# Freeing 8 KB of tables, more buffers for two kinds of tile, a new order for the first weight slab and spaced loads, in a fused long-convolution and gated-MLP training step

## Chip, cores and metric

One core of one Trainium2 chip. The time is the device time of one execution in microseconds (us). The kernel before took 2044.09 us (median of 3 runs, 2042.13 to 2049.22) when the prediction was made.

## The reference

Forward and backward pass of one block, for 2048 positions, 1024 channels and an MLP width of 3584, all in bf16. The output and the gradients of nine inputs are wanted.

```python
xn = layernorm(q)
k_shift = sum of 4 shifted copies of k, each times a column of shift_k
kv = k_shift * v
y = irfft(rfft(pad(kv)) * rfft(pad(ssm_k)))[:2048] + kv * ssm_D      # long convolution
s = xn * y
h = (xn @ w_gate) * (xn @ w_up)
g = silu(h @ w_down)
out = q + s * g
# and jax.vjp of this with respect to q, k, v, shift_k, ssm_k, ssm_D, w_gate, w_up, w_down
```

## The kernel before

TensorE does the large products. The convolution runs beside them: its Fourier transforms are small matmuls with table tiles (TF for one direction, TI for the other) plus additions on VectorE, fed to the engines a piece at a time while the matmul loops go on. `tt` is a two-input VectorE instruction, `ld` a load issued by SyncE, `sta` a store issued by ScalarE, and `st` and `cld` a store and a load issued by GpSimd. Tiles come from pools. In the profile's lines a name that ends in d (DYFd, HFd, DGd) is a tensor in device memory, a name that begins with ps is a tile in PSUM, and U stands for any tile of the pool from which dgu comes.

```python
TI = tip.tile([P, 2, 8, 2, P], BF16, name="TI")      # 8 KB a partition
TF = tfp.tile([P, 2, 8, 2, P], BF16, name="TF")      # 8 KB; the second halves are needed only in the forward convolution
# ... the first two weight slabs (chunks of 1, 1, 2, 4, 4, 4 row blocks):
for i, (b0, n, x4) in enumerate(xs):
    # ... layer norm of the next chunk
    for sl in range(2):
        gu_unit(sl, b0, n, slabs[sl], nop)
# ... backward, gradient of h for one half of a slab:
def dh_half(k, wdt):
    for g in range(2):
        dht = bg.tile([P, 4, SLW], BF16, name="dht", bufs=3)
        for e in range(2):
            # ... 16 matmuls into ps
            nc.scalar.copy(out=dht[:, 2 * e:2 * e + 2]..., in_=ps[:])
            flush(2)                                  # runs stores deferred earlier
            btick(1)                                  # lets the backward convolution go on a little
        tt(dgu[:, bs], dgu[:, bs], dht..., MUL)
    def store():                                      # two DMAs from ScalarE's queue
        for a in range(2):
            sta(DGd[...], dgu[:, :, a, :])
    defer(store)
# ... backward convolution:
def conv_backward():
    cx, cs = pool("d_cx", 2), pool("d_cs", 1)
    yield from dy_forward(cx, cs)      # 8 units: load kvx and dyx, transform into DX (in d_cs), store DYFd[ds] <- DX
    cs.release(); cx.release(); tfp.release()
    ab, cs, ew = pool("e_ab", 1), pool("e_cs", 1), pool("e_ew", 1)
    # A and B: two tiles of 8 KB each
    load_a(0)                          # A <- DYFd[0]
    load_b(0)                          # B <- HFd[0]
    for n in range(16):                # product of A and B, inverse transform, tail
        yield from staggered(main(n), tl, 5.0)
        tl = tail(n)
```

Of the kernel before, what the change touches and what calls it, by code (L numbers as in the profile page):

```python
# [13 lines left out]
BF16 = mybir.dt.bfloat16  # L14
# [5 lines left out]
def build_kernel(  # L20
# [11 lines left out]
    nc = tc.nc  # L32
    P = 128
# [6 lines left out]
    SLW = 256  # L40
# [17 lines left out]
    V = nc.vector  # L58
# [66 lines left out]
    Wbc = const.tile([P, 4, D], BF16, name="Wbc")  # L125

    tip = tc.alloc_tile_pool(name="tip", bufs=1)
    TI = tip.tile([P, 2, 8, 2, P], BF16, name="TI")
    tfp = tc.alloc_tile_pool(name="tfp", bufs=1)
    TF = tfp.tile([P, 2, 8, 2, P], BF16, name="TF")  # L130
    T4 = [TF[:, 0], TF[:, 1]]

    def zero_rows(bsb):
        zr = bsb.tile([8, 8, P], BF16, name="zr")
# [31 lines left out]
    def build_tables(psp, tg, ang):  # L166

        m = ang
        for q in range(2):
            dst = T4[q].rearrange("p r k f -> p k r f")  # L170
            sc = 2.0 * np.pi / 4096.0
            mm = tg.tile([P, 8, P], I32, name="mm")
            if q == 0:
                V.tensor_single_scalar(mm[:], m[:], 4095, ALU.bitwise_and)
            else:
                nc.gpsimd.iota(mm[:], pattern=[[512 * q, 8], [0, P]], base=0, channel_multiplier=0)
                tt(mm[:], m[:], mm[:], ADD)
                V.tensor_single_scalar(mm[:], mm[:], 4095, ALU.bitwise_and)
            nc.scalar.activation(dst[:, 1], mm[:], ACT.Sin, bias=negpi[:], scale=sc)
            ab_ = tg.tile([P, 8, P], F32, name="ab_")  # L180
            nc.scalar.activation(ab_[:], mm[:], ACT.Abs, bias=negpi[:], scale=sc)
            nc.scalar.activation(dst[:, 0], ab_[:], ACT.Sin, bias=mhpi[:], scale=1.0)
        for j in range(2):
            for rq in range(2):
                ps = psp.tile([P, 4, 2, P], BF16, name="tr")
                for i in range(4):
                    for k in range(2):
                        nc.tensor.transpose(ps[:, i, k, :], T4[j][:, 4 * rq + i, k, :], ident[:])
                V.tensor_copy(TI[:, j, 4 * rq:4 * rq + 4], ps[:])


    def pr(t, i, j):
# [154 lines left out]
    def gseg(G, r, j, k):  # L347
        a = r % 4
        return G[:, 4 * a + 2 * j + (1 - k if a == 3 else k), :]
# [37 lines left out]
    def inv8_rows(G, psp, rp):  # L387
        ps = psp.tile([P, 2, 256], F32, name="psY")
        for i in range(2):
            r = 2 * rp + i  # L390
            for k in range(2):
                nc.tensor.matmul(ps[:, i, :], TI[:, 0, r, k, :], G[:, 2 * r + k, :], start=(k == 0), stop=(k == 1))
        return ps

    def inv_rows(G, psp, rp):

        ps = psp.tile([P, 2, 256], F32, name="psY")
        for i in range(2):
            r = 2 * rp + i
            n = 0  # L400
            for j in range(2):
                for k in range(2):
                    nc.tensor.matmul(ps[:, i, :], TI[:, j, r, k, :], gseg(G, r, j, k),
                                     start=(n == 0), stop=(n == 3))
                    n += 1
        return ps
# [172 lines left out]
    def conv_forward():  # L579
# [96 lines left out]
        kst.release()  # L676
        cs.release()
        cx.release()

    F_TOTAL = 4 * 20.0 + 8 * (0.2 + 2 * FWD4_W + 1.4 + 1.2 + PROD_W + INV_W + 1.6)  # L680
    nop = lambda: None
# [21 lines left out]
    for i, (b0, n, x4) in enumerate(xs):  # L703
        if i + 1 < len(xs):
            with tc.issue_after(last.ins):
                last, root, xst = layer_norm(*xs[i + 1])
        for sl in range(2):
            gu_unit(sl, b0, n, slabs[sl], nop)
            if i in (3, 4):
                with tc.issue_after(gu_mm[0].ins):  # L710
                    for j in ((3, 4), (2,), (1,), (0,))[2 * (i - 3) + sl]:
                        bcast(j)
        if i == len(xs) - 1:
            with tc.issue_after(root.ins):
                build_tables(ps_st, tg, ang)
# [184 lines left out]
    def dh_tail(ds, G, ew):  # L900
        hr = ew.tile([P, 2, 8, P], BF16, name="yl")
        ho = ew.tile([P, 2, P, 8], BF16, name="ho")
        for c in range(2):
            for rq in range(2):
                ps = ps_y4[0].tile([P, 4, P], F32, name="psY")
                for i in range(4):
                    r = 4 * rq + i
                    for k in range(2):
                        nc.tensor.matmul(ps[:, i, :], G[:, 2 * r + k, c * P:(c + 1) * P], TI[:, 0, r, k, :],
                                         start=(k == 0), stop=(k == 1))  # L910
                nc.scalar.activation(hr[:, c, 4 * rq:4 * rq + 4], ps[:], ACT.Copy, scale=WSC)
                yield 0.1
        nc.gpsimd.tensor_copy(ho[:], hr[:].rearrange("p c r u -> p c u r"))
        st(o_dssmk[ds * P:(ds + 1) * P, :], ho[:].rearrange("p c u r -> p (c u r)"))
        yield 0.1

    def dk_units(ew, psp):
        def load(i):
            ds, c = divmod(i, 2)
            kh = ew.tile([P, 11, P], BF16, name="kh")  # L920
            cld_k(kh[:], c, ds)
            dk = ew.tile([P, 11, P], BF16, name="dkh")
            src = DKSHd[ds]
            cld(dk[:], bass.AP(src.tensor, src.offset + 1024 * c * P, [[8 * P, P], [P, 11], [1, P]]))
            return kh, dk

        kh, dk = load(0)
        yield 2
        for i in range(16):
            ds, c = divmod(i, 2)  # L930
            dsl = slice(ds * P, (ds + 1) * P)
            wb = lambda j: Wbc[:, j:j + 1, dsl].to_broadcast([P, 8, P])
            acc = ew.tile([P, 8, P], BF16, name="dka")
            tt(acc[:], dk[:, 3:11, :], wb(3), MUL)
            for j in (2, 1, 0):
                prod = ew.tile([P, 8, P], BF16, name="dkp")
                tt(prod[:], dk[:, j:j + 8, :], wb(j), MUL)
                tt(acc[:], acc[:], prod[:], ADD)
                yield 1
            st(o_dk[:, c, :, dsl], acc[:])  # L940
            if c == 0:
                ps = psp.tile([P, 4, 64], F32, name="psdk")
            for r in range(8):
                for j in (slice(0, 64), slice(64, 128)):
                    nc.tensor.matmul(ps[j], dk[:, r, j], kh[:, r:r + 4, j],
                                     start=(c == 0 and r == 0), stop=(c == 1 and r == 7))
            yield 1
            if i < 15:
                kh, dk = load(i + 1)
            if c == 1:  # L950
                dt_ = ew.tile([P, 4, 64], F32, name="dt2")
                tt(dt_[:], ps[:], diag[:].unsqueeze(1).to_broadcast([P, 4, 64]), MUL)
                dr_ = ew.tile([P, 4], F32, name="dr2")
                V.tensor_reduce(dr_[:], dt_[:], AX.X, ADD)
                V.tensor_copy(dsko[:, ds, ::-1], dr_[:])
            yield 2
        st(o_dshk.rearrange("(c p) j -> p c j", p=P), dsko[:])
    DK_TOTAL = 2 + 16 * 6

# [122 lines left out]
    def dh_half(k, wdt):  # L1082

        sl, hf = divmod(k, 2)
        dgu = DGU[k]
        for g in range(2):
            bs = slice(4 * g, 4 * g + 4)
            dht = bg.tile([P, 4, SLW], BF16, name="dht", bufs=3)
            for e in range(2):
                ps = ps_b.tile([P, 512], F32, name="psb")  # L1090
                for x in range(2):
                    b = 4 * g + 2 * e + x
                    for dc in range(DC):
                        nc.tensor.matmul(ps[:, x * SLW:(x + 1) * SLW], DBMT[2 * hf + g][:, dc, (b % 4) * P:(b % 4 + 1) * P],  # L1094
                                         wdt[:, dc, :], start=(dc == 0), stop=(dc == DC - 1))
                nc.scalar.copy(out=dht[:, 2 * e:2 * e + 2].rearrange("p b f -> p (b f)"), in_=ps[:])  # L1096
                flush(2)
                btick(1)
            with tc.high_priority(60):
                tt(dgu[:, bs], dgu[:, bs], dht[:].unsqueeze(2).to_broadcast([P, 4, 2, SLW]), MUL)  # L1100

        def store():
            fs = slice(sl % 2 * SLW, sl % 2 * SLW + SLW)
            for a in range(2):
                sta(DGd[sl // 2, a, 1024 * hf:1024 * hf + 1024, fs].rearrange("(b u) f -> u b f", u=P), dgu[:, :, a, :])
        defer(store)
        return dgu
# [49 lines left out]
    for p_ in (bg, bw):  # L1157
        p_.release()
    gd2 = pool("gd2", 1, side="right")
    wo = pool("wo", 4, side="right")  # L1160



# [199 lines left out]
```

## Time and profile before

| stage (where it starts) | us in the profile before |
|---|---|
| layer norm, slabs 0 and 1, start of slab 2, forward convolution | 0 to 569.0 |
| down projection | 569.0 to 767.0 |
| gradient of h, gradients of gate and up weights, backward convolution | 767.0 to 1426.7 |
| gradient of the down weight | 1426.7 to 1626.1 |
| gradient of x | 1626.1 to 2030.0, tail to 2039.6 |

The marks are the start of the first instruction of each stage on its main tile. The prediction shows the busy times by stage and the waits. Columns of single profile lines: start, duration, engine, instruction, idle time ahead of it and what ended that.

```profile
966.67 0.55 POOL L65 DMA_DIRECT2D DYFd<-DX  x1 [17.63 <-DVE DX L242]
967.45 0.54 POOL L65 DMA_DIRECT2D A<-DYFd  x1 [0.24 <-issue]
967.98 0.54 POOL L65 DMA_DIRECT2D B<-HFd  x1
968.51 0.53 POOL L65 DMA_DIRECT2D A<-DYFd  x1
977.30 0.53 POOL L65 DMA_DIRECT2D B<-HFd  x1 [8.27 <-DMA DYFd<-DX]
```

### The profile page before, as it was taken

What the parts mean: (1) busy time and instruction counts of PE and PEld (TensorE: products, weight loads), DVE (VectorE), ACT (ScalarE), POOL (GpSimd) and SP (SyncE); (2) the same over time, 40 slices, a digit from 0 to 9 for tenths busy, and PEclk for the clock granted to TensorE, in tenths of its full rate; (3) what the DMA queues carried; (4) which work ended last, traced back from release to release, by engine and by line L of the source; (5) the groups of instructions that cost most, each with busy time, mean ns of one, the idle gap of its engine ahead of it and who ended that gap; (6) DMA issues with size and microseconds to landing.
All of it is one profiled execution on the core that took longest, in us unless ns stands there. A gap on an engine that the chain in (4) does not pass through costs nothing.

```text
span 2039.6 us, 28672 instructions
## 1 busy us (share of the span) xinstructions
PE 1953.3 (96%) x11345; PEld 1053.9 (52%) x11530; DVE 1485.6 (73%) x2007; ACT 607.2 (30%) x956; POOL 341.8 (17%) x499
## 2 busy tenths in 40 slices
PE   6999999999999999999998999999999999999998
PEld 3455555555544446666565555565444444444443
DVE  7789999999836555888899899998968024444343
ACT  4644444444432233322222222222222101111112
POOL 3322222221112111000122111112121001111100
PEclk9999999999999999999999999999999999999999
DMA  9686766558699988766889778866996989393921
GB/s 302 233 289 209 249 219 229 196 199 276 213 304 291 292 282 277 228 210 172 296 246 250 224 221 265 249 202 223 244 234 167 219 207 225 102 219 92 232 69 57
DMA packets 468711, 454.43 MB, mean 223 GB/s; under 512 B 249456, under 2 KB 393624, under 8 KB 454624
## 3 DMA queue, kind: packets, MB, share of 16 engines
q1 hardware_dynamic: 324240, 190.08, 36.6%
q0 software_dynamic: 45200, 189.08, 27.4%
q10 hardware_dynamic: 99136, 73.42, 11.5%
q8 instruction: 90, 1.47, 0.3%
q14 instruction: 45, 0.37, 0.1%
HBM read 208.15 MB, written 194.02 MB: 197 GB/s over the span
## 4 chain that ended last, share of the span: by engine, by line
PE 60%; DVE 22%; issue 9%; DMA 6%; POOL 1%; ACT 1%; ACTq 0%; SPq 0%; DVEq 0%; POOLq 0%
PE psx L1235 19%; PE psbm L969 9%; PE psb L1212 9%; PE psb L1113 9%; DVE W L198 6%; DVE m L198 6%; PE psg L556 6%; PE psb L1094 3%; DVE HX L198 2%; DVE U L198 1%; DVE KX L198 1%; DMA B<-HFd 1%; DMA dyl<-DYd 1%; DVE A L198 1%; DVE B L198 1%
## 5 line engine op out<-in xcount | busy, mean ns | idle before, releaser
L556 PE MATMUL psg<-wslab,U 128*128 128x512 bf16 x1732 | 408.1, 382 | 11.8 <-ACT U L530 3.6
L1113 PE MATMUL psb<-U,U 128*128 128x512 bf16 x1745 | 399.9, 384 | 11.8 <-ACT dht L1096 5.4
L1235 PE MATMUL psx<-U,dgut 128*128 128x512 bf16 x1503 | 332.4, 379 | 2.8 <-issue 1.4
L1113 PEld LDWEIGHTS <-U 128*128 128x128 bf16 x1792 | 176.8, 99 | 216.1 <-issue 19.6
L1235 PEld LDWEIGHTS <-dgut 128*128 128x128 bf16 x1792 | 173.8, 98 | 211.1 <-issue 3.7
L556 PEld LDWEIGHTS <-U 128*128 128x128 bf16 x1792 | 173.6, 98 | 195.8 <-issue 12.6
L1094 PE MATMUL psb<-wdt,U 128*128 128x256 bf16 x1792 | 203.8, 274 | 10.8 <-ACT dht L1096 9.6
L558 ACT CAST gut<-psg 128x512 bf16<-128x512 f32 x224 | 131.2, 587 | 228.3 <-PE psg L556 212.0
L1212 PE MATMUL psb<-U,U 128*128 128x512 bf16 x876 | 194.8, 379 | 1.1
L1094 PEld LDWEIGHTS <-U 128*128 128x128 bf16 x1792 | 175.8, 98 | 34.6 <-issue 11.4
L969 PE MATMUL psbm<-U,ht 128*128 128x512 bf16 x768 | 168.9, 379 | 0.8
L1117 ACT CAST wb<-psb 128x512 bf16<-128x512 f32 x112 | 65.6, 586 | 317.0 <-PE psb L1113 229.0
L198 DVE TENSOR_TENSOR W<-W 128x1024 f32<-128x1024 f32 (+1 forms) x144 | 142.8, 1010 | 2.8
L198 DVE TENSOR_TENSOR m<-A,B 128x1024 bf16<-128x1024 bf16 (+1 forms) x160 | 116.6, 793 | 32.9 <-issue 23.3
L1212 PEld LDWEIGHTS <-U 128*128 128x128 bf16 x896 | 87.1, 98 | 102.4
L198 DVE TENSOR_TENSOR dka<-dkh,Wbc 128x1024 bf16<-128x1024 bf16 x16 | 11.1, 692 | 163.2 <-DMA dkh<-DKSHd 163.2
L969 PEld LDWEIGHTS <-ht 128*128 128x128 bf16 x784 | 76.6, 98 | 91.8
L1258 ACT ACTIVATE dx_t<-dxn 128x1024 bf16<-128x1024 f32 (+1 forms) x17 | 17.1, 1007 | 339.1 <-DVE dxn L198 285.8
L1096 ACT CAST dht<-psb 128x512 bf16<-128x512 f32 x112 | 65.0, 587 | 152.7 <-PE psb L1094 103.8
L198 DVE TENSOR_TENSOR W<-W,psP 128x512 f32<-128x512 f32 x128 | 81.0, 692 | 8.6 <-ACT W L228 6.7
L198 DVE TENSOR_TENSOR U<-U,dht 128x2048 bf16<-128x2048 bf16 x56 | 70.4, 1258 | 21.5 <-ACT dht L1096 21.5
L1214 ACT CAST wbs<-psb 128x512 bf16<-128x512 f32 x56 | 32.8, 586 | 159.5 <-PE psb L1212 142.4
(233 smaller groups left out, 2335.3 us busy)
## 6 DMA issues: line engine op xcount, KB each, us to landing
U<-GUd SPq DMA_DIRECT2D x28, 1024.0 KB, 7.2
DGd<-U ACTq DMA_DIRECT2D x56, 512.0 KB, 6.6
GUd<-gut ACTq DMA_DIRECT2D x54, 512.0 KB, 4.8
A<-DYFd POOLq DMA_DIRECT2D x16, 1024.0 KB, 5.5
U<-Hd SPq DMA_DIRECT2D x15, 1024.0 KB, 6.1
out_dram<-wb ACTq DMA_DIRECT2D x224, 64.0 KB, 3.3
Hd<-hN POOLq DMA_DIRECT2D x54, 256.0 KB, 4.0
HTd<-hT POOLq DMA_DIRECT2D x54, 256.0 KB, 4.2
```

What stands on the lines that cost most here:

```text
L198: V.tensor_tensor(o, a, b, op)
L556: gu_mm[0] = nc.tensor.matmul(ps[:], XNT[q][:, dc, qi * P:(qi + 1) * P], w[:, dc].rearrange("p a f -> p (a f)"), start=(dc == 0), stop=(dc ...
L558: nc.scalar.copy(out=gut[:, i].rearrange("p a f -> p (a f)"), in_=ps[:])
L969: nc.tensor.matmul(ps[:, dh * 512:(dh + 1) * 512], ht(fc)[:, i * P:(i + 1) * P], WD[fc // 4][:, fc % 4, dh * 512:(dh + 1) * 512], start=(f ...
L1094: nc.tensor.matmul(ps[:, x * SLW:(x + 1) * SLW], DBMT[2 * hf + g][:, dc, (b % 4) * P:(b % 4 + 1) * P], wdt[:, dc, :], start=(dc == 0), sto ...
L1096: nc.scalar.copy(out=dht[:, 2 * e:2 * e + 2].rearrange("p b f -> p (b f)"), in_=ps[:])
L1113: nc.tensor.matmul(ps[:], XN[b // 4][:, b % 4, dc * P:(dc + 1) * P], dgus[b // 8][:, b % 8].rearrange("p a f -> p (a f)"), start=(b == 0), ...
L1117: nc.scalar.copy(out=wb[:].rearrange("p a f -> p (a f)"), in_=ps[:])
L1212: nc.tensor.matmul(ps[:], h[:, b, f * P:(f + 1) * P], DBM[b // 4][:, b % 4, dh * 512:(dh + 1) * 512], start=(b == 0), stop=(b == NB - 1))
L1214: nc.scalar.copy(out=wbs[:, dh * 512:(dh + 1) * 512], in_=ps[:])
L1235: nc.tensor.matmul(ps[:, dh * 512:(dh + 1) * 512], t[n][:, f, i * P:(i + 1) * P], WGU[n][:, f, dh * 512:(dh + 1) * 512], start=(n == 0 and ...
L1258: nc.scalar.activation(dx_t[:, cl], dxn[:, cl], ACT.Identity, accum_out=sums[:, 0, h:h + 1])
```

## The change

Its intent: the second halves of TI and TF are given to a pool of their own (tfo) that is released after the forward convolution, which frees 8 KB a partition; the room goes to two more buffers for dht and two for the stores of the down gradient (wbs). The two units of slab 0 are put ahead of the last units of slab 1, so that its buffer comes free sooner. The work units of the dk part are weighted anew, so that a load has more time before its first use.

```diff
-    TI = tip.tile([P, 2, 8, 2, P], BF16, name="TI")
+    TI = [tip.tile([P, 8, 2, P], BF16, name="TI0")]
     tfp = tc.alloc_tile_pool(name="tfp", bufs=1)
-    TF = tfp.tile([P, 2, 8, 2, P], BF16, name="TF")
-    T4 = [TF[:, 0], TF[:, 1]]
+    T4 = [tfp.tile([P, 8, 2, P], BF16, name="TF0")[:]]
+    tfo = tc.alloc_tile_pool(name="tfo", bufs=1)
+    TI.append(tfo.tile([P, 8, 2, P], BF16, name="TI1"))
+    T4.append(tfo.tile([P, 8, 2, P], BF16, name="TF1")[:])
 ...  (each TI[:, j, ...] becomes TI[j][:, ...])
         cx.release()
+        tfo.release()
 ...
-        for sl in range(2):
-            gu_unit(sl, b0, n, slabs[sl], nop)
-            if i in (3, 4):
+        for sl, c in ([(0, i), (1, i)], [(0, i)], [(0, i), (1, i - 1), (1, i)])[max(0, i - len(xs) + 3)]:
+            gu_unit(sl, xs[c][0], xs[c][1], slabs[sl], nop)
+            if c in (3, 4):
 ...  (dk: yields of 1, 1 and 2 become 0.5, 0.5 and 4)
-            dht = bg.tile([P, 4, SLW], BF16, name="dht", bufs=3)
+            dht = bg.tile([P, 4, SLW], BF16, name="dht", bufs=5)
 ...
-    wo = pool("wo", 4, side="right")
+    wo = pool("wo", 6, side="right")
```

More of the change, by code (lines that the diff above doesn't have):

```diff
@@ L188, in build_tables @@
                         nc.tensor.transpose(ps[:, i, k, :], T4[j][:, 4 * rq + i, k, :], ident[:])
-                V.tensor_copy(TI[:, j, 4 * rq:4 * rq + 4], ps[:])
+                V.tensor_copy(TI[j][:, 4 * rq:4 * rq + 4], ps[:])
     def pr(t, i, j):
@@ L391, in inv8_rows @@
             for k in range(2):
-                nc.tensor.matmul(ps[:, i, :], TI[:, 0, r, k, :], G[:, 2 * r + k, :], start=(k == 0), stop=(k == 1))
+                nc.tensor.matmul(ps[:, i, :], TI[0][:, r, k, :], G[:, 2 * r + k, :], start=(k == 0), stop=(k == 1))
         return ps
@@ L402, in inv_rows @@
                 for k in range(2):
-                    nc.tensor.matmul(ps[:, i, :], TI[:, j, r, k, :], gseg(G, r, j, k),
+                    nc.tensor.matmul(ps[:, i, :], TI[j][:, r, k, :], gseg(G, r, j, k),
                                      start=(n == 0), stop=(n == 3))
@@ L706, in build_kernel @@
                 last, root, xst = layer_norm(*xs[i + 1])
-        for sl in range(2):
-            gu_unit(sl, b0, n, slabs[sl], nop)
-            if i in (3, 4):
+        for sl, c in ([(0, i), (1, i)], [(0, i)], [(0, i), (1, i - 1), (1, i)])[max(0, i - len(xs) + 3)]:
+            gu_unit(sl, xs[c][0], xs[c][1], slabs[sl], nop)
+            if c in (3, 4):
                 with tc.issue_after(gu_mm[0].ins):
-                    for j in ((3, 4), (2,), (1,), (0,))[2 * (i - 3) + sl]:
+                    for j in ((3, 4), (2,), (1,), (0,))[2 * (c - 3) + sl]:
                         bcast(j)
@@ L908, in dh_tail @@
                     for k in range(2):
-                        nc.tensor.matmul(ps[:, i, :], G[:, 2 * r + k, c * P:(c + 1) * P], TI[:, 0, r, k, :],
+                        nc.tensor.matmul(ps[:, i, :], G[:, 2 * r + k, c * P:(c + 1) * P], TI[0][:, r, k, :],
                                          start=(k == 0), stop=(k == 1))
@@ L938, in dk_units @@
                 tt(acc[:], acc[:], prod[:], ADD)
-                yield 1
+                yield 0.5
             st(o_dk[:, c, :, dsl], acc[:])
@@ L946, in dk_units @@
                                      start=(c == 0 and r == 0), stop=(c == 1 and r == 7))
-            yield 1
+            yield 0.5
             if i < 15:
@@ L955, in dk_units @@
                 V.tensor_copy(dsko[:, ds, ::-1], dr_[:])
-            yield 2
+            yield 4
         st(o_dshk.rearrange("(c p) j -> p c j", p=P), dsko[:])
```

## The prediction

> **What bounds the kernel now.** I read the page's busy shares first, then the busy time of each engine by stage, then the list of waits on TensorE, then the order of instructions around the three largest gaps. From the page:
>
> ```profile
> PE 1953.3 (96%) x11345; PEld 1053.9 (52%) x11530; DVE 1485.6 (73%) x2007; ACT 607.2 (30%) x956; POOL 341.8 (17%) x499
> ```
>
> TensorE is busy for 1953.3 of 2039.6 us, so only 86.3 us of idle time can be won, plus whatever is lost to matmuls that run slower after a gap. The table by stage (columns: stretch, its length, busy time of PE, PEld, DVE, ACT, POOL, granted clock, DMA share, GB/s) says where that idle time lies. I cut the stages at the layer norm with the first two weight slabs, the start of slab 2, the other twelve slabs with the forward convolution, the down projection, the gradients of h and of gate and up with the backward convolution, the gradient of down, the gradient of x, and the tail:
>
> ```profile
> 0.00:96.40 96.40, 77.11 (x467) 37.90 (x474) 69.11 (x164) 59.52 (x88) 33.47 (x59) 1.00 0.80 262
> 96.40:116.00 19.60, 16.07 (x83) 7.77 (x85) 15.62 (x17) 5.93 (x10) 7.47 (x12) 0.91 1.05 344
> 116.00:569.40 453.40, 433.43 (x2702) 248.66 (x2753) 424.37 (x566) 217.26 (x344) 96.76 (x148) 1.00 0.66 229
> 569.40:765.00 195.60, 193.51 (x900) 88.80 (x918) 105.58 (x167) 51.69 (x51) 39.35 (x62) 1.00 0.95 292
> 765.00:1423.00 658.00, 630.19 (x4153) 387.76 (x4200) 580.12 (x729) 171.82 (x302) 97.55 (x141) 0.98 0.76 234
> 1423.00:1626.00 203.00, 201.94 (x1047) 96.96 (x1065) 131.07 (x151) 43.26 (x77) 28.68 (x20) 1.00 0.92 220
> 1626.00:2030.00 404.00, 400.75 (x2003) 186.02 (x2038) 155.23 (x206) 54.72 (x80) 38.53 (x61) 1.00 0.68 154
> ```
>
> Length minus PE busy: 19.3, 3.5, 20.0, 2.1, 27.8, 1.1 and 3.3 us; the tail of 9.6 us holds another 9.3. The two stages of the four edits that come last (down's gradient, x's gradient) have 4.4 us of idle between them. The stage with the gradient of h has most, and the granted clock is below one there and at the start of slab 2. The waits on TensorE:
>
> ```profile
> PE psb L1094 <- ACT dht L1096: 9.6, 2, 8.2
> PE psY L403 <- DVE HX L198: 9.0, 8, 2.0
> ...
> PE psb L1113 <- ACT dht L1096: 5.4, 1, 5.4
> ...
> PE psg L556 <- DMA wslab<-in_B_w_gate_dram: 3.3, 1, 3.3
> ```
>
> So what the change aims at on the path is 9.6 + 5.4 us behind ScalarE's copy into dht and 3.3 us behind one slab load.
>
> **What the Trainium skill says, and whether the trace agrees.** "TensorE: Matmul & The Clock Gate", Part 1 (the HAM clock gate), says that an idle window of about 3.4 us sends the array back to half clock and that about 3.4 us of work brings it back. The trace agrees: after the 5.43 us gap at 1170 fifteen records of 512 columns take from 1175.7 to 1181.8 us, 6.1 us, where warm ones are 0.216 us apart (49 in 10.74 us on the chain) and would need 3.2: 2.9 us lost beside the gap. "PSUM — Partial Sum Buffer", Engine vs sequencer instructions, says the queues of ScalarE and VectorE are strict FIFO; the ScalarE lines below agree, as four results sit in or wait for PSUM behind a store. "Perfetto Trace Analysis", Identifying Performance Opportunities, says that a gap that repeats on the engine that should be saturated can mean too few buffers. Here I doubt that reading, as I show next. "DMA: Bandwidth & Descriptors", Queues, rings and completion order, says each DMA engine takes turns among its queues; slab 2's load, in company with two 512 KB copies of k, takes 11.8 us, against a median of 7.1 for the 28 slab loads.
>
> **The change part by part.**
>
> First slab sooner. Before, the blocks of the last chunk follow the order slab 0 chunk 4, slab 1 chunk 4, slab 0 chunk 5, slab 1 chunk 5; slab 0's buffer comes free only at 87.3 us, and its successor is issued then:
>
> ```profile
> 87.32 0.39 SPq L480 DMA_DIRECT2D wslab<-in_B_w_up_dram  x1
> 87.75 0.59 SPq L480 DMA_DIRECT2D wslab<-in_B_w_gate_dram  x1
> ```
>
> It lands at 99.55; TensorE has run out at 96.4. After, both slab 0 units come first. A unit of four blocks is 32 matmuls, 32 x 0.216 = 6.9 us (with its transposes about 7.5), so the load starts near 80 and lands near 92 even at 11.8 us. The 3.25 us gap goes. Behind it, eight matmuls and eight transposes take 3.6 us where 2.2 would do: 1.4 us more. 4.7 us in sum. But from 116 us VectorE is busy 424.4 of 453.4 us, and TensorE's small gaps there are waits for it (9.0 us for HX). VectorE must also start the convolution sooner for TensorE to keep its lead; it idles 3.7 us near 103 for a store of shifted k that competes with the slab load, so I expect it to move most of the way. I put 4.0 us.
>
> Five dht buffers. Round the 8.19 us gap ScalarE and VectorE do this:
>
> ```profile
> 1110.16 0.59 ACT L1096 CAST dht<-psb 128x512 bf16<-128x512 f32 x1 [1.16 <-PE psb L1094]
> 1122.48 0.39 ACTq L68 DMA_DIRECT2D DGd<-U  x1
> 1122.91 0.59 ACT L1096 CAST dht<-psb 128x512 bf16<-128x512 f32 x1 [12.17 <-DVE U L198]
> ```
>
> ```profile
> 1112.43 1.23 DVE L198 TENSOR_TENSOR dyl<-dyl,Dbc 128x2048 bf16<-128x2048 bf16 x1 [4.15 <-DMA dyl<-DYd]
> 1113.57 2.28 DVE L198 TENSOR_TENSOR W<-A 128x2048 f32<-128x2048 bf16 x1
> ...
> 1118.29 1.22 DVE L198 TENSOR_TENSOR U<-U,dht 128x2048 bf16<-128x2048 bf16 x1
> ```
>
> The fifth cast does not wait for a dht buffer: with three, it takes the one whose product was made a whole slab earlier. It stands in ScalarE's queue behind the store of the product (DGd), which needs the second product of VectorE, done at 1122.45; and VectorE is late because of a load of dy. The same order (casts, store, cast) stands at the 5.43 us gap. Two more buffers remove the wait of the seventh cast for the first product, which this store already covers. They help only if the program's order around the store changes with them. If the store moves behind the casts, TensorE would go on to the weight gradients at 1117 and still need the product that ends at 1122.45 for its twelfth block, some 4 us of waiting in place of 8.2; at the other gap, where the second product ends at 1174.6 and TensorE would want it at 1170.3 + 12 x 0.216 = 1172.9, about 1.7 in place of 5.4. With the slow clocks behind the gaps (1.5 + 2.9 us) and the 1.4 us gap at 1309 that is 4.2 + 3.7 + 4.4 + 1.4 = 13.7 us at best. I give it somewhat under one half: 6.0 us.
>
> More down-store buffers: the gradient of down idles 1.1 us in 203. Worth 0, at most 1 us.
>
> dk's loads spaced. VectorE waits 163.2 us for dkh, the largest wait of the kernel, but TensorE idles 3.3 us in that stage of 404 us. The pump turns 98 units in about 196 x 1.73 = 339 us, 3.46 us a unit; the first product moves from two units after its load (6.9 us) to four (13.8 us), beyond the longest landing of 12.3 us. The wait should fall a great deal and the time not at all. The last 9.6 us hold no dk work. Worth 0.
>
> Sum: 4.0 + 6.0 + 0.5 (the small waits) = 10.5 us, from 2044.1 to 2033.6.
>
> **The rivals.** (1) The order of ScalarE's queue stays, the two long gaps stay: then only the slab's 4 us remain, 2040. For it speaks the store at 1122.48; against it, that a larger buffer count lets the instruction order be drawn up anew. (2) VectorE becomes the bound: in the convolution stages it is at 94% and 88%. Then TensorE's earlier start turns into longer waits for HX, and moved products meet later DMA loads: 2044, or with an unlucky order 2050. For it speaks the 9.0 us of HX waits in eight equal parts, one for each slice of channels; against it, that VectorE has ended its convolution near 553 us, some 15 us before TensorE ends that stage. (3) The new order also heals the gaps that no edit names: the 7.84 us for which a store holds ScalarE's queue at 784 us (3.7 us idle and 3.1 of slow clock), the 2.0 us at 994 with 1.9 of slow clock. Then the time would be near 2020.
>
> **Range and chances.** All idle time but the first 8 us and the tail is 69 us, and faster by over 2% would need 41 of it; none of the edits reaches that. Slower by over 2% would need an order much worse than this one in a kernel whose idle time is spread thin. Range 2020 to 2045: the lower end is rival 3, the upper is rival 2.
>
> **What would show it.** Slab 2's load issued near 80 us and no TensorE wait for it: step one right. DVE's first product of the convolution no earlier than 118 us would make it worth nothing. The waits of psb for dht gone while the DGd store still stands between casts would show me wrong on the queue; gaps of 5 to 8 us still there with DGd at their end would show me right, and the time near 2040. VectorE's wait for dkh below 60 us with PE idle still near 3 us in the last stage: the dk step right. An idle sum of the stage from 765 us above 28 us would make the whole prediction too low.

## More of the kernel before

Pools on the left side of SBUF form a stack that grows upwards, pools on the right one that grows downwards, and a pool's address is wherever the stack stands when it is opened.

```profile
970.39 1.23 DVE L198 TENSOR_TENSOR U<-U,dht 128x2048 bf16<-128x2048 bf16 x1 [4.01 <-ACT dht L1096]
973.88 1.23 DVE L198 TENSOR_TENSOR U<-U,dht 128x2048 bf16<-128x2048 bf16 x1 [2.27 <-ACT dht L1096]
977.38 1.22 DVE L198 TENSOR_TENSOR U<-U,dht 128x2048 bf16<-128x2048 bf16 x1 [2.27 <-ACT dht L1096]
982.21 3.63 DVE L198 TENSOR_TENSOR m<-A,B 128x2048 bf16<-128x2048 bf16 x5 [3.61 <-DMA B<-HFd]
```

The first B is asked for at 967.98 and used at 982.21. The second B, at 977.30, waits 8.27 us for the last store of DX. Nothing in the program's data joins B and DX: that wait is about the room they lie in.

## The result, and the profile after

The changed kernel took 2059.85 us (median of 4 runs, 2057.57 to 2061.37); the kernel before took 2045.21 us in the same rounds (4 runs, 2042.13 to 2049.22). The ratio is 1.0069, with a 95% interval of 1.0048 to 1.0091. All ratios here are the mean time of one kernel's fast runs over the mean of the other's fast runs of the same rounds, so not quite the ratio of the medians quoted. The change is within 2%, but it is slower, where 10.5 us faster was predicted, and it lies 15 us above the range's upper end.

The marks of the two profiled runs, in us:

| | down projection | gradient of h | down gradient | gradient of x | length of the stage from "gradient of h" |
|---|---|---|---|---|---|
| before | 569.0 | 767.0 | 1426.7 | 1626.1 | 659.7 |
| after | 571.2 | 769.1 | 1443.8 | 1643.2 | 674.7 |

Of 17.1 us by which the gradient of x starts later, 15.0 arise in the stage with the gradient of h. The table by stage of the changed kernel (columns as in the prediction's) puts that down to idle time of TensorE:

```profile
96.40:116.00 19.60, 19.41 (x140) 11.29 (x141) 14.36 (x15) 8.56 (x13) 6.57 (x10) 1.00 0.99 321
116.00:571.60 455.60, 433.29 (x2679) 247.30 (x2728) 431.90 (x573) 215.28 (x341) 98.22 (x150) 1.00 0.66 229
...
767.20:1440.10 672.90, 630.41 (x4153) 387.93 (x4200) 580.03 (x729) 171.21 (x302) 96.78 (x141) 0.97 0.76 229
```

In the third line TensorE is busy for 630.41 us, as before (630.19), and idle for 672.90 - 630.41 = 42.5 us, before 27.8: 14.7 us more. The list of waits on TensorE names where (columns: line, releaser, us in total, times, longest):

```profile
PE psb L1117 <- ACT wb L1121: 14.5, 1, 14.5
...
PE psb L1098 <- ACT dht L1100: 8.3, 2, 7.6
...
PE psY L394 <- DVE B L244: 5.6, 1, 5.6
PE psb L1117 <- ACT dht L1100: 4.7, 3, 4.0
```

The waits behind dht, which the change was to remove, are still there (8.3 + 4.7 for 9.6 + 5.4). New is one wait of 14.5 us behind ScalarE's cast into wb, the tile in which a block of a weight gradient is stored. It is followed back through four engines. TensorE, then ScalarE, then VectorE, then GpSimd's queue, of the changed kernel:

```profile
1008.91 12.98 PE L1117 MATMUL psb<-U,U 128*128 128x512 bf16 x47 [14.51 <-ACT wb L1121]
```

```profile
1007.21 1.02 ACTq L68 DMA_DIRECT2D DGd<-U  x2
1008.28 0.58 ACT L1121 CAST wb<-psb 128x512 bf16<-128x512 f32 x1 [23.61 <-DMA out_dram<-wb]
```

```profile
977.76 1.23 DVE L200 TENSOR_TENSOR U<-U,dht 128x2048 bf16<-128x2048 bf16 x1 [2.27 <-ACT dht L1100]
1000.00 3.63 DVE L200 TENSOR_TENSOR m<-A,B 128x2048 bf16<-128x2048 bf16 x5 [21.02 <-DMA B<-HFd]
1003.56 1.28 DVE L200 TENSOR_TENSOR m<-m 128x1024 bf16<-128x1024 bf16 x2
1004.76 1.28 DVE L200 TENSOR_TENSOR A<-m 128x1024 bf16<-128x1024 bf16 x2
1005.96 1.22 DVE L200 TENSOR_TENSOR U<-U,dht 128x2048 bf16<-128x2048 bf16 x1
```

```profile
967.05 0.54 POOL L65 DMA_DIRECT2D DYFd<-DX  x1 [17.64 <-DVE DX L244]
967.59 0.53 POOL L65 DMA_DIRECT2D A<-DYFd  x1
977.65 0.53 POOL L65 DMA_DIRECT2D B<-HFd  x1 [9.53 <-DMA DYFd<-DX]
978.17 0.53 POOL L65 DMA_DIRECT2D A<-DYFd  x1
978.69 0.53 POOL L65 DMA_DIRECT2D B<-HFd  x1
979.24 0.53 POOL L65 DMA_DIRECT2D dyl<-DYd  x1
979.88 2.98 POOL L65 DMA_DIRECT2D vl<-in_A_v_dram  x4
```

Read from below. The load of the first B now waits 9.53 us for the last store of DX, and is issued at 977.65 for 967.98. Behind it seven loads (A, B, dyl and four of vl) go out in one burst. B is usable only at 1000.00, 22 us after its issue, for 14 us before, and VectorE stands still for 21.02 us in front of a product that needs it, where it waited 3.61. Behind that product, in VectorE's order, stands the fourth product of U with dht (1005.96); the store of U (DGd, 1007.21) needs it; ScalarE's casts stand behind the store (1008.28; the profile puts the wait down to an old store of wb, but the DGd store just ahead of the cast ran 1 us before, right after the product's end at 1007.18); and TensorE's next matmuls need a PSUM tile that those casts empty (1008.91).

Why B waits for DX is shown by no profile but by the addresses in the compiled programs (bytes in a partition):

```
tile               before                          after
TI / TF            28288-36480 / 36480-44672       28288-32384 / 32384-36480
dyx (2 buffers)    52864-61056                     44672-52864
DX                 61056-69248                     52864-61056
A, first           36480-44672                     32384-40576
B, first           52864-61056  (on dyx)           48768-56960  (on dyx and DX)
B, second          61056-69248  (on DX)            56960-65152  (on DX)
```

The pools of the eight forward units stand on top of TI and TF, so they move down by the freed 8 KB. The pool of A and B stands in place of TF itself, so it moves down by 4 KB. Against each other they are shifted by 4 KB, and the first B comes to lie partly on DX. Before, only the second B did, whose product follows the first without a gap. The load of B into room that the store of DX still reads waits for that store: 9.53 us here.

### The profile page after: what moved, and what is told of

The parts are those of the page before. It is cut to its first block, busy times and chain, and to the rows that moved or that the text cites. A ratio compares the mean times of both kernels' runs of the same rounds, so it can differ in the third digit from the quotient of the medians.

```text
span 2056.8 us, 28643 instructions
## 1 busy us (share of the span) xinstructions
PE 1957.1 (95%) x11346; PEld 1055.1 (51%) x11530; DVE 1488.2 (72%) x2007; ACT 606.8 (30%) x956; POOL 340.2 (17%) x499
## 4 chain that ended last, share of the span: by engine, by line
PE 57%; DVE 24%; issue 11%; DMA 6%; POOL 1%; ACT 1%; ACTq 1%; SPq 0%; DVEq 0%; POOLq 0%
PE psx L1239 18%; PE psbm L973 9%; PE psb L1216 9%; DVE W L200 7%; PE psg L558 6%; DVE m L200 6%; PE psb L1117 5%; DVE HX L200 3%; PE psb L1098 3%; DVE U L200 2%; DVE KX L200 1%; DMA vl<-in_A_v_dram 1%; DMA dyl<-DYd 1%; PE psY L405 1%; DVE B L200 1%
## 5 line engine op out<-in xcount | busy, mean ns | idle before, releaser
L1117 PE MATMUL psb<-U,U 128*128 128x512 bf16 x1745 | 399.9, 384 | 23.5 <-ACT wb L1121 14.5
L1098 PEld LDWEIGHTS <-U 128*128 128x128 bf16 x1792 | 175.8, 98 | 33.3 <-issue 10.1
L200 DVE TENSOR_TENSOR dka<-dkh,Wbc 128x1024 bf16<-128x1024 bf16 x16 | 11.1, 692 | 183.1 <-DMA dkh<-DKSHd 183.1
L1262 ACT ACTIVATE dx_t<-dxn 128x1024 bf16<-128x1024 f32 (+1 forms) x17 | 17.1, 1007 | 338.5 <-DVE dxn L200 297.7
```

Of the source, the lines that this page charges most:

```text
L200: V.tensor_tensor(o, a, b, op)
L1098: nc.tensor.matmul(ps[:, x * SLW:(x + 1) * SLW], DBMT[2 * hf + g][:, dc, (b % 4) * P:(b % 4 + 1) * P], wdt[:, dc, :], start=(dc == 0), sto ...
L1117: nc.tensor.matmul(ps[:], XN[b // 4][:, b % 4, dc * P:(dc + 1) * P], dgus[b // 8][:, b % 8].rearrange("p a f -> p (a f)"), start=(b == 0), ...
```

## The experiments

Medians are in us. Before ran at 2047.97 (11 runs) beside e1 to e4, at 2046.14 (11) beside e5 to e8, and at 2049.28 (11) beside e9 and e10; each of these groups ran on another chip, so ratios are compared across groups and not medians. "Stage" is the length of the stage with the gradient of h in the profiled run, by the marks of the first table.

| run | median (runs) | ratio, 95% interval | stage |
|---|---|---|---|
| before | 2045.21 (4) | 1 | 659.7 |
| after | 2059.85 (4) | 1.0069 (1.0048 to 1.0091) | 674.7 |
| e1, before, tables split only | 2063.49 (4) | 1.0064 (1.0032 to 1.0096) | 671.0 |
| e2, after, 4 KB of padding | 2051.75 (4) | 1.0008 (0.9971 to 1.0045) | 666.8 |
| e3, after, three dht buffers | 2064.00 (4) | 1.0057 (1.0018 to 1.0095) | 673.2 |
| e4, before, slab order only | 2046.77 (6) | 0.9986 (0.9960 to 1.0012) | 660.2 |
| e5, after, DX elsewhere | 2043.44 (6) | 0.9982 (0.9959 to 1.0004) | 657.9 |
| e6, e5 with a later DGd store | 2045.23 (6) | 0.9987 (0.9961 to 1.0012) | 658.9 |
| e7, e6 with three dht buffers | 2043.84 (6) | 0.9985 (0.9964 to 1.0007) | 661.5 |
| e8, before, dk and wbs edits only | 2045.12 (4) | 0.9987 (0.9961 to 1.0013) | 663.2 |
| e9, three dht buffers, first A and B loaded ahead | 2036.42 (6) | 0.9947 (0.9919 to 0.9976) | 653.7 |
| e10, e9 with a later DGd store | 2031.58 (6) | 0.9928 (0.9895 to 0.9961) | 643.6 |

The theory was that the shift of the tiles makes the loss. The rivals were that one of the named edits does: another order of instructions from five dht buffers, or VectorE's new order from the slab edit.

**e1: the kernel before with nothing but the split tables.**

```diff
  before, with TI and TF cut in halves and tfo released, as in the change; dht 3 buffers, wo 4, slab and dk as before
```

> The kernel before with the tables alone split in halves and the second halves freed early; four table and loop edits of the change left out otherwise, and the built order of the instructions is that of before but for three table copies on VectorE. Theory P (placement): the freed room moves every tile behind the tables down by 4 or 8 KB, so that the first buffer for the spectra (B) no longer lies where the dead loads of dy lay but on DX, whose last store must be read out first; the load of B is issued about 9 us later, in one burst with four others. P expects about 2059 us, ratio 1.006 to 1.009, with the 14 us wait of the weight gradients behind ScalarE near 994 us. Rival Q (the five buffers or the other loop edits cost the time): 2045 us, ratio 1.000.

The order of instructions is that of the kernel before on four engines, and differs in 3 lines on VectorE. The whole loss is there: ratio 1.0064. The list of waits of this run in the stage, on TensorE:

```profile
PE psb L1097 <- ACT dht L1099: 8.4, 2, 7.7
PE psb L1116 <- ACT wb L1120: 7.1, 1, 7.1
PE psY L394 <- DVE B L244: 6.2, 1, 6.2
```

The wait behind wb is half as long as in the changed kernel, but the same chain. So the loss comes with freeing the room, not with what the room was used for.

**e2: the changed kernel with 4 KB of padding below the forward units**, which undoes the shift between DX and B and leaves all else.

```diff
+        pd = pool("d_pad", 1)
+        pd_t = pd.tile([P, 2048], BF16, name="padding")
+        V.memset(pd_t[:, 0:2], 0.0)
         cx = pool("d_cx", 2)
```

> The changed kernel with an unused 4 KB tile put ahead of the dy loads, so that B lies on the dy loads again and DX on B's second buffer, as before; the order of instructions is that of the changed kernel but for one tiny memset. P expects the 14.5 us and 5.6 us waits of TensorE near 1000 us gone and 2043 to 2047 us, ratio 0.998 to 1.002. Q: 2059, ratio 1.007.

The 14.5 us wait is gone (3.5 us are left behind wb, and 4.4 of the 5.6 us behind B), and most of the loss with it: the ratio is 1.0008, and all four runs lie below all four of e1. The expected 2043 to 2047 us were missed, though. The median is 3.8 us above that of the kernel before, which the interval doesn't tell from nothing. The padding moved dyx too, to 48768, onto a tile of the gate (dbm, 47072 to 51168) whose store had just been issued. The next two lists are GpSimd's issues and TensorE's waits of e2:

```profile
784.02 0.54 POOL L65 DMA_DIRECT2D dyx<-DYd  x1 [7.88 <-DMA DBMd<-dbm]
```

```profile
PE psY L809 <- DMA dyx<-DYd: 10.5, 1, 10.5
```

It is the same fault at another place: 10.5 us of TensorE waiting for a load that waits for a store it has nothing to do with. What that wait costs in time was not measured alone.

**e3: the changed kernel with three dht buffers.**

```diff
-            dht = bg.tile([P, 4, SLW], BF16, name="dht", bufs=5)
+            dht = bg.tile([P, 4, SLW], BF16, name="dht", bufs=3)
```

> The changed kernel with three dht buffers in place of five; the built order of instructions is identical on all five engines. P, and my claim that the store in ScalarE's queue and not the buffers is what blocks the casts: no change against the changed kernel, 2059 us, ratio 1.006 to 1.009. If the buffers had helped at all: slower than the changed kernel, 2065. If they were what cost the time: 2045.

The compiled order is the same in every line on all five engines with three buffers and with five. The ratio, 1.0057 (runs of 2051.89 to 2068.03), cannot be told from the 1.0069 of five, and TensorE's waits behind dht are 8.2 + 4.5 us with three and 8.3 + 4.7 with five. The two buffers did not make the loss, and nothing shows that they brought anything.

**e4: the kernel before with the slab order alone.**

```diff
  before, with the loop over (sl, c) of the change in place of the loop over sl
```

> The kernel before with only the new order of the slab units. My prediction put this at -4 us (2041, ratio 0.998). The rival that VectorE bounds the convolution stage: slab 2's load lands in time and TensorE's 3.3 us wait goes, but the first product of the convolution on VectorE starts no sooner than 118 us and the end of the stage stays at 569 us: 2045, ratio 0.999 to 1.001. From the changed kernel's one trace it could also be +2, ratio 1.001, if its reordered VectorE queue starts the convolution later.

Ratio 0.9986, and the interval holds 1: a gain of at most 8 us (0.4%), and not shown; the predicted 4 us (0.2%) lie within the interval too. It isn't the cause of the loss.

**e5: the changed kernel with DX in a pool above the rest**, on room that neither A, B nor an unfinished store uses (77728 to 85920).

```diff
         cs = pool("d_cs", 1)
-        yield from dy_forward(cx, cs)
+        dxp = pool("d_dx", 1)
+        yield from dy_forward(cx, cs, dxp)
 ...
-            X = cs.tile([P, 16, 256], BF16, name="DX")
+            X = dxp.tile([P, 16, 256], BF16, name="DX")
```

> The changed kernel with DX (the spectrum of dy) in a pool of its own behind the work tiles, clear of both B buffers, and the dy loads left low, where the 4 KB pad had pushed the first of them onto the gate's output tiles, whose store made TensorE wait 10.5 us. The built order is nearly that of the changed kernel (12 rows of 23062 differ on TensorE, 60 of 1389 on VectorE). Theory P: both placement waits gone (B near 994 us, dyx near 786 us), some 8 us better than the padded kernel: 2042 to 2046 us, ratio 0.997 to 1.000. If P is wrong about the pad's second wait: 2051, ratio 1.002 or above.

GpSimd's issues in this run:

```profile
968.56 0.54 POOL L65 DMA_DIRECT2D DYFd<-DX  x1 [17.63 <-DVE DX L244]
969.10 0.53 POOL L65 DMA_DIRECT2D A<-DYFd  x1
969.85 0.53 POOL L65 DMA_DIRECT2D B<-HFd  x1 [0.21 <-issue]
```

B is issued at once, the stage is 657.9 us long, and the time is 2043.44. One tile at another address takes back the whole loss, with every edit of the change still in place. The profiles agree. In the three kernels whose first B lies on DX (after, e1, e3) its load waits 9.5 to 10.4 us for the store, and VectorE then stands still for 21.0, 13.6 and 19.1 us in front of the first product; in before, e2 and e4 to e8 it stands there for 3.6 to 9.7 us. What all edits are worth together without the fault is 0.9982, an interval that holds 1.

**e6 and e7: e5 with the DGd store moved behind the casts it stood in front of, with five and with three dht buffers.** This tests the prediction's picture of the waits behind dht.

```diff
+                cast[0] = nc.scalar.copy(out=dht[...], in_=ps[:])      # likewise for the casts into wb
 ...
             for a in range(2):
-                sta(DGd[...], dgu[:, :, a, :])
+              with tc.issue_after(cast[0].ins):
+                sta(DGd[...], dgu[:, :, a, :])
-        defer(store)
+        later.append([-3, store])
```

> The former kernel with the store of the products (DGd) held in ScalarE's queue behind the casts of the next half and the first weight-gradient cast. My prediction's claim that the store and not the buffer count blocks the casts: the two waits behind dht (8 and 4 us) shrink to those for the product itself, some 9 us with the slow clock behind them; 2034 to 2038, ratio 0.993 to 0.996. If the claim is wrong: equal to e5.

> The former kernel with three dht buffers; the built order is identical on all engines. Now that no store stands ahead of the seventh cast, that cast meets the buffer of the first product of the same slab: if the two more buffers are of any use, this is the place, and the kernel is 1 to 5 us slower than e6. If not: equal to e6 within 2 us.

The waits behind dht, 11.3 + 0.7 us in e5, left the list of e6's stage, and others of the same size took their place. TensorE's waits in e6:

```profile
PE psb L1122 <- DVE U L200: 9.1, 4, 4.0
PE psY L394 <- DVE B L244: 8.8, 1, 8.8
PE psb L1122 <- ACT wb L1126: 3.6, 1, 3.6
```

In this profile, then, the store was where VectorE's lateness showed, not what made TensorE wait. TensorE now waits for the same product of VectorE without ScalarE between. The predicted 2034 to 2038 us were missed: the median is 2045.23 for 2043.44, though the runs are spread from 2038.23 to 2050.91 and the profiled one is the slowest. In e7, whose order equals e6's in every line, no use of the buffers is seen even then (ratio 0.9985 for 0.9987).

**e8: the kernel before with the dk weights and six wbs buffers alone.**

```diff
  before, with the yields 0.5, 0.5 and 4 of the change, and wo with 6 buffers
```

> The kernel before with only dk's loads spaced and six down-store buffers. My prediction: no change in the time (ratio 0.999 to 1.001), and VectorE's wait for dkh down from 163 us to below 60. The trace of the changed kernel already speaks against the second: there it is 183 us. Reading it as mere idleness of an engine whose next instruction happens to be that one, I now expect 160 to 190 us of wait and an unchanged time, 2047.

Ratio 0.9987, and the interval holds 1. VectorE's wait in front of the instructions that read dkh is 180.6 us, and 163.2 in the kernel before. The room itself never came. From the issue of a dkh load to the first product that reads it the median of the 16 is 5.4 us before and 5.5 in e8, about the time that such a load takes to land (median 5.3 and 5.4). VectorE stands at that product before the load has landed, so the units of work that the program puts between the two don't set the distance here.

**e9 and e10: what would really help VectorE.** Even before the change it idles for 4.01 + 2.27 + 2.27 + 3.61 = 12.2 us ahead of the first product: the last 3.61 for the load of B, the rest for casts into dht, whose products stand ahead in VectorE's order. In e9 the room is laid out by hand. The first A and B get 16 KB of their own below the pools of the forward units, so that they can be loaded after the sixth of the eight units; DX and dyx lie on room that nobody is storing from. Three dht buffers are what fits. e10 adds the later store of e6.

```diff
-        cx = pool("d_cx", 2)
-        cs = pool("d_cs", 1)
-        yield from dy_forward(cx, cs)
+        ab = [pool("e_ab0", 1)]                       # A and B of the even units
+        cs, cx, dxp = pool("d_cs", 1), pool("d_cx", 2), pool("d_dx", 1)
+        yield from dy_forward(cx, cs, dxp, lambda: (load_a(0), load_b(0)))   # called after unit 5
 ...
-        cs.release(); cx.release(); tfp.release()
-        ab = pool("e_ab", 1)
+        dxp.release(); cx.release(); cs.release()
+        ab.append(pool("e_ab1", 1))                   # A and B of the odd units; tfp is kept to the end
-        load_a(0)
-        load_b(0)
```

> The changed kernel with three gradient buffers, and the first spectrum pair of the backward convolution (8 KB of DYF and 8 KB of HF) loaded after the sixth of the eight forward units into two tiles of their own below everything else, instead of after the last one; DX lies on the dead input tiles. VectorE idled about 11 us at 967 to 984 us even in the kernel before, waiting for that pair, and is 99% busy from there to about 1590 us. Theory (VectorE's lateness is what the gaps behind psb, wb and psY between 1000 and 1240 us come from): VectorE's first product starts within 2 us of its last forward addition, TensorE's gaps over 3 us between 970 and 1240 us, some 25 us in the kernel before and 20 in e5, fall to under 10, and the time falls to 2028 to 2036, ratio 0.991 to 0.996. Rival (the gaps come from the order on ScalarE or from DMA traffic): the idle time of VectorE goes, the gaps stay, and the time is 2040 to 2045, ratio 0.997 to 1.000.

> e9 with the store of DGd issued behind the casts that it held up (the edit of e6). Theory (both the idle time of VectorE and the store's place cost): 3 to 5 us below e9, at 2025 to 2032. Rival (with VectorE early the product U is ready when the store's turn comes, so the place of the store is free): the same as e9 within 2 us.

VectorE at the join in e9:

```profile
965.28 1.28 DVE L244 SCALAR_TENSOR_TENSOR DX<-W 128x512 bf16<-128x512 f32 x2
966.59 3.63 DVE L200 TENSOR_TENSOR m<-A,B 128x2048 bf16<-128x2048 bf16 x5
```

The product follows the last forward addition at once, 966.59 for 982.21 before; the products with dht now come after it in VectorE's order, so that the edit changed that order as well as the load. (The expected "99% busy" was a misreading: in the kernel before VectorE is busy for 541.95 of the 606 us from 984 to 1590, 89%.) The ratio of e9 is 0.9947, below 1 with its whole interval, and the stage is 6.0 us shorter than before. TensorE's waits over 3 us between 960 and 1260 fell from 8.2 + 5.4 us to 4.1 + 3.6. (My "some 25" for the kernel before was its sum of all waits over the whole stage, 24.8; the same sum is 19.9 in e9.) e10 is the fastest kernel: 2031.58 us, ratio 0.9928, stage 643.6. Its waits on TensorE over the whole stage are

```profile
PE psb L1124 <- DVE U L200: 8.3, 6, 2.5
PE psP L217 <- DVE W L200: 2.8, 2, 2.3
PE psP L217 <- DVE ddo L815: 0.4, 1, 0.4
```

11.5 us for 24.8, none longer than 2.5. The edit of the store that showed nothing in e6 shortens the stage by 10.1 us here and lowers the median by 4.8. (The two profiled runs differ by 2.8 us only: e10's began the stage 2.3 us later and took 5.0 us longer for the gradient of x.) The intervals of e9 and e10 overlap: five runs of e10 lie at 2029.33 to 2033.92 and one at 2049.18; four of e9 lie at 2033.39 to 2036.57 and two at 2043.35 and 2043.79. That the late store adds to e9 is thus seen in the profile and in most runs, and isn't settled by the times.

## Why the prediction was wrong

**The term that was left out.** This is the step that failed: the sum had four terms, one for each named edit, and none for what made room for two of them. "Five buffers in room freed from the tables" was read as what the buffers do, not as what freeing 8 KB does to everything stacked on it. The e1 run is that missing term by itself: ratio 1.0064, about 13 us on 2046; e5, which puts DX elsewhere and keeps the rest, is its reverse. The trace of before had the hint, since the second B waited 8.27 us for DX's store there. I had looked at GpSimd's issues in seven other stretches, one from 980 us on, but not in this one, because no edit touched them.

**"First slab sooner … I put 4.0 us."** The mechanism was half right. Slab 2's load is issued at 81.47 (near 80 was expected, 87.32 before), and TensorE's 3.3 us wait for it is gone: idle 0.2 us in the window of 96.4 to 116, 3.5 before. The other half, that VectorE moves most of the way, failed. The issue and then VectorE in the changed kernel:

```profile
81.47 0.39 SPq L482 DMA_DIRECT2D wslab<-in_B_w_up_dram  x1
```

```profile
89.45 0.69 DVE L200 TENSOR_TENSOR hN<-gut 128x1024 bf16<-128x1024 bf16 x1 [6.66 <-ACT gut L560]
...
116.01 1.23 DVE L200 TENSOR_TENSOR U<-k,Wbc 128x2048 bf16<-128x2048 bf16 x1 [3.76 <-DMA KSHd<-U]
...
120.15 1.28 DVE L200 TENSOR_TENSOR W<-W,psP 128x512 f32<-128x512 f32 x2
```

It meets a wait of 6.66 us for a copy of the reordered units and, as before, one of 3.76 us for a store of shifted k, and its first addition of a convolution transform starts at 120.15, before at 118.09. That is past the 118 us at which I had called the step worth nothing. More profiles say the same: the first addition starts at 119.6 to 120.2 us in after and e2 to e5, which have the edit, and at 118.1, 121.0 and 120.0 in before, e1 and e8, which have not; the down projection starts at 568.0 to 571.7 us in all nine profiles with the edit and at 569.0 to 574.0 in the three without. The 22.3 us for which TensorE is idle in the convolution stage, 20.0 before, can thus not be put down to the edit. Alone (e4) the edit is worth 0.14%, told neither from nothing nor from the 4.0 us. The profiled run of after also has a spell of low clock (0.54 from 51 to 56 us); so has that of e8 (0.50 from 50.5 to 55.5), where this part of the kernel is as before.

**"Five dht buffers … I give it somewhat under one half: 6.0 us."** No gain was measured (e3, e7). The reading of the queue was right: with five buffers the casts wait as long as with three. The hope that "a larger buffer count lets the instruction order be drawn up anew" was an addition against my own evidence, and e3 and e7 show not one line of the order changed. The waits stand with DGd at their end, as rival 1 has it. ScalarE around the longest, in the changed kernel:

```profile
1129.34 0.59 ACT L1100 CAST dht<-psb 128x512 bf16<-128x512 f32 x1 [1.16 <-PE psb L1098]
1141.12 0.39 ACTq L68 DMA_DIRECT2D DGd<-U  x1
1141.55 0.58 ACT L1100 CAST dht<-psb 128x512 bf16<-128x512 f32 x1 [11.62 <-DVE U L200]
```

The estimate that a later store would turn 8.2 us into "some 4 us" and 5.4 into 1.7 failed too in e6: it took VectorE's times as fixed. Waits that short came about only when VectorE had been made earlier (e10).

**"More down-store buffers … 0" and dk "the time not at all".** Nothing speaks against either (e8, ratio 0.9987, an interval that holds 1). "The wait should fall a great deal" was wrong: it rose to 183.1 us in the changed kernel. The step that failed is "3.46 us a unit": four units were to be 13.8 us after the load, but VectorE runs ahead of that pace, and the first product follows the load by 5.6 us (median of 16 in the changed kernel). In the last stage VectorE is idle for 404.00 - 155.23 = 248.8 us before and 404.00 - 155.15 = 248.9 after; only what the profile puts this idle time down to has changed.

**"An idle sum of the stage from 765 us above 28 us would make the whole prediction too low."** It was 42.5 us. **Rival 2** came nearest, by luck, with its "2050 with an unlucky order" and "moved products meet later DMA loads", but it made VectorE's load the cause, and the cause was one address. (Its "eight equal parts" were misread: eight waits for HX sum to 9.0 us, the longest 2.0.) The upper end of the range, 2045, left no room for a part that the argument had not seen.

**What stays open.** e1 shows a 7.1 us wait where after shows 14.5, and both lose about the same time; TensorE's waits in the stage sum to 36.2 us in e1, 39.7 in after and 24.8 before. In e1 the same burst of loads goes out, and B is usable 14.0 us after its issue (984.89 to 998.87), as before the change. The burst alone thus doesn't make the 22 us of after; what does was not found. e8's profiled stage of 663.2 us, with an unchanged time, shows that a single profiled stage can be some 3 us off.

## What to carry to other kernels

Where tiles are placed by a stack of pools, freeing room is a change of its own: list the addresses of all later tiles before and after, and for each load into reused room ask which store read it last. A gap behind a queued store is worth only as much as the producer behind that store is early; look one engine further before moving the store. When the engine that feeds the others stands idle at the join of two stages, loading the next stage's first operands one or two units ahead can be worth more than buffers inside a stage.

## What the Trainium skill lacked or had wrong

- "SBUF — State Buffer" gives sizes, ports and alignment, but says nothing of the cost of two tiles sharing an address one after the other. Here the load of B waited 9.53 us for the store of a dead tile, and the stage grew by 15.0 us; with padding the load of dyx waited 7.88 us for another and TensorE 10.5.
- "Perfetto Trace Analysis", Identifying Performance Opportunities, offers too few buffers as a reading of a repeated gap. Here three and five buffers give the same order in every line, and the gaps of 8.2 and 5.4 us became 7.6 and 4.0 us; waits of that size went only with an earlier VectorE and a later store together (none over 2.5 us in e10).
- I found no page that warns that a long wait of an engine with time to spare is mere idleness: VectorE's wait for dkh was 163.2 us before and 183.1 after, and TensorE's idle time in that stage 3.3 and 404.00 - 400.59 = 3.4 us.
- "TensorE: Matmul & The Clock Gate", Part 1, ties half clock to an idle window of about 3.4 us. The trace of before agreed behind its 5.43 us gap. In the profiled run of after the clock is 0.54 from 51 to 56 us, and the longest gap of TensorE in the 11 us ahead is 1.14 us. The same part of the page tells of short idles that do this in another kernel; what set this spell off was not followed up.
